# Fused block-causal attention and hash-routed experts on one core: V and rest casts moved to Pool, mask and rest-exponential work merged

## The chip, the cores and the metric

The kernel runs on one core of a Trainium2 chip (trn2). A core has a matmul engine (TensorE, PE in the profile, with its weight loads shown apart as PEld), a vector engine (VectorE, DVE), an activation engine (ScalarE, ACT), a programmable engine (GpSimd, POOL) and a queue engine for transfers (SyncE, SP). Each engine works through its own instructions strictly in program order, and engines wait for one another through semaphores. The metric is the device time of one execution in microseconds (us).

## The reference

Two stages follow each other. The first is block-causal attention over 8 batches of 8 heads, 576 positions and 64 dimensions per head; position blocks are 64 long, and a query sees its own block and all earlier ones. The second sends each of the 4608 resulting rows (512 wide, all heads of a position side by side) through one of 8 experts, chosen by a hash of its token id.

```
scores = scale * q @ k^T            # per batch and head, 576 x 576
scores = where(block_i >= block_j, scores, -1e9)
attn   = softmax(scores);  y = attn @ v
x      = y as [8*576 rows, 512]
e      = token_ids * 2654435761 % 8
out[row] = relu(x[row] @ w1[e]) @ w2[e]   # w1: 512 x 1024, w2: 1024 x 512
```

## The kernel before

**Attention.** Work goes in 32 pairs of heads, numbered g = 4*b + pr for batch b and pair pr. The 576 positions are 512 "main" positions, taken as four tiles of 128, and a "rest" of 64 (the last block). q, k and v come in as float32 by `load_qk` and `load_v` on SP's transfer queue (the first q and k partly on ACT's), into tiles `qf`, `kf`, `vf` with two buffers each. They are cast to bf16: q and k by `cast_qk` (L161) on DVE, two pairs at a time, and their rests of all heads at L174 in one cast; v by `cast_v` (L176) for one pair at a time. `cast_v` makes the four main tiles on DVE (L181, 128 partitions x 512 elements) and two "half block" tiles, which gather 64-row pieces on other partitions, on Pool (L182 and L183, 64 x 256 each). `cast_v4` (L185) puts the rest of V of the whole batch into `v4` on Pool (L189, twice 64 x 256). `vx` and `v4` have two buffers, chosen by the parity of the batch.

`T_pair` (L212) transposes q and k of one pair on PE and DVE copies the result (L231); `T_rest` (L195) does so for the rests of a whole batch. `S_chunk` (L270) makes one third of a pair's scores in PSUM and ACT takes their exponential (L286); there are two such PSUM buffers (`psS`). `mm_mask` (L257) adds a large negative number where a block may not be seen, by a rank-one matmul of `maskk` and `maskq`. For the key tile of half blocks (argument c true) it issues four matmuls of 64 x 64 tiles: two halves x of the output partitions times two heads m. `S_rest` (L288) makes the rest-by-rest scores of all heads of a batch: eight 64 x 64 matmuls, head m in PSUM bank m, and then two exponentials of 64 x 256 (L301), because the two heads lie in different banks. `PV` (L316) multiplies with V, 15 matmuls for each head of the pair; its PSUM tile has one buffer (`psO`). `norm` (L336) divides by the sums on DVE (L343, L346). `write_x` (L353) writes a finished batch to HBM in bf16 with five transfers that Pool issues (L356 four times, L358 once), since later rows are gathered by index.

**The order of the work** is written out by hand in the loop at L564 over g = 0 to 33. Iteration g has, in program order: the scores of pair g, interleaved with `PV` and `norm` of pair g-2; `T_pair(g + 2)`; `cast_v(g - 1)`, with `cast_v4` at the first pair of a batch (L588 to L592); one step of `steps`; a quarter of the casts of the next batch (L595 to L604), the q rest at pr 0, the k rest at pr 1 and `T_rest(b + 1)` at pr 2; at pr 1 `write_x(b - 1)`; then the loads: `load_qk(b + 2)`, and at pr 0 `load_v(b + 1)`. So V of pair g is cast in iteration g+1 and used by `PV` in iteration g+2.

**Routing** rides along in `steps`. Iterations 2 to 8 compute each token's slot, mainly on DVE. From iteration 10 each batch j has `place_a` at g = 10+2j (one-hot tiles `ohp` and `ohs` on DVE at L490 and L493, products `ohg` on Pool at L496 and L499) and `place_b` at g = 11+2j (five matmuls on PE at L509, which wait for `ohg`). Iterations 6 to 15 each clear one gather buffer on Pool (L612).

**Experts.** From L688 on, Pool gathers 128 rows at a time by index (L632), PE transposes them (L644) and does both matmuls (L656, L671), and Pool scatters the results (L678). A loop at L710 for rows over an expert's capacity comes last. Nothing in this part is edited.

Of the kernel before, what the change touches and what calls it, by code (L numbers as in the profile page):

```python
# [8 lines left out]
ACT = mybir.ActivationFunctionType  # L9
AX = mybir.AxisListType  # L10
F32 = mybir.dt.float32
BF16 = mybir.dt.bfloat16
# [8 lines left out]
B, H, S, D = 8, 8, 576, 64  # L21
# [3 lines left out]
NP = H // 2  # L25
# [4 lines left out]
NEG = -30000.0  # L30
SCALE = 1.0 / float(D) ** 0.5
# [3 lines left out]
def kernel(  # L35
# [10 lines left out]
    nc = tc.nc  # L46
    P = nc.NUM_PARTITIONS

    const = ctx.enter_context(tc.tile_pool(name="const", bufs=1))
# [9 lines left out]
    identbf = const.tile([P, P], BF16, name="identbf")  # L59
    lower = const.tile([P, P], BF16, name="lower")  # L60
    onesbf = const.tile([P, P], BF16, name="onesbf")
    maskk = const.tile([P, P], BF16, name="maskk")
    maskq = const.tile([P, P], BF16, name="maskq")
    perm3 = const.tile([P, NG], I32, name="perm3")
    xgs = [const.tile([P, DM], BF16, name=f"xg{z}") for z in range(2 * G)]
# [11 lines left out]
    nc.vector.memset(maskq[:], 0.0)  # L77
    for m in range(2):
        row = slice(64 * m, 64 * m + 1)
        nc.vector.memset(maskk[row, 96:128], NEG)  # L80
        nc.vector.memset(maskq[row, :], 1.0)

    att_ctx = ExitStack()
# [11 lines left out]
    def load_qk(b, h0=0, h1=H, rest=True, main=True, engs=None):  # L95
        if b not in loaded:
            loaded[b] = [ld.tile([P, 36, D], F32, name="qf", tag="qf"),
                         ld.tile([P, 36, D], F32, name="kf", tag="kf"), None]
        for w, src in ((0, q), (1, k)):
            t = loaded[b][w]  # L100
            eng = engs[w] if engs else nc.sync
            if main and w == 0:
                eng.dma_start(
                    t[:, 4 * h0 : 4 * h1, :].rearrange("p (h c) d -> p h (c d)", c=4),
                    src[b, h0:h1, 0:512, :].rearrange("h (p c) d -> p h (c d)", c=4),
                )
            elif main:
                for r in range(2):
                    eng.dma_start(
                        t[:, 4 * h0 : 4 * h1, :].rearrange(  # L110
                            "p (h r c) d -> p h r (c d)", r=2, c=2)[:, :, r],
                        src[b, h0:h1, 256 * r : 256 * r + 256, :].rearrange("h (p c) d -> p h (c d)", c=2),
                    )
            if rest:
                for g in range(2):
                    eng.dma_start(
                        t[64 * g : 64 * g + 64, 32:36, :],
                        src[b, 4 * g : 4 * g + 4, 512:576, :].rearrange("h r d -> r h d"),
                    )
# [18 lines left out]
    for z in range(2):  # L138
        vx = fix.tile([P, H, 6, D + 1], BF16, name=f"vx{z}")
# [21 lines left out]
    def cast_qk(b, which, r0=0, r1=NP, rest=True):  # L161
        src = loaded[b][which]
        cb = casted.setdefault(b, {})
        if which not in cb:
            cb[which] = att.tile([P, 36, D], BF16, name="qb" if which == 0 else "kb",
                                 tag="qb" if which == 0 else "kb")
        dst = cb[which]
        if r1 > r0:
            nc.vector.tensor_copy(  # L169
                dst[:, 8 * r0 : 8 * r1, :].rearrange("p (r c m) d -> p r m c d", c=4, m=2),  # L170
                src[:, 8 * r0 : 8 * r1, :].rearrange("p (r m c) d -> p r m c d", c=4, m=2),
            )
        if rest:
            nc.vector.tensor_copy(dst[:, 32:36, :], src[:, 32:36, :])  # L174

    def cast_v(b, pr):  # L176
        vf = loaded[b][2]
        vx, v4 = vexts[b % 2]
        hs = slice(2 * pr, 2 * pr + 2)
        vm = vf[:, 0:32, :].rearrange("p (h s) d -> p h s d", h=H)  # L180
        nc.vector.tensor_copy(vx[:, hs, 0:4, 0:D], vm[:, hs])  # L181
        nc.gpsimd.tensor_copy(vx[0:64, hs, 4:6, 0:D], vm[0:64, hs, 0::2, :])  # L182
        nc.gpsimd.tensor_copy(vx[64:128, hs, 4:6, 0:D], vm[0:64, hs, 1::2, :])  # L183

    def cast_v4(b):  # L185
        vf = loaded[b][2]
        vx, v4 = vexts[b % 2]
        for m in range(2):
            nc.gpsimd.tensor_copy(  # L189
                v4[64 * m : 64 * m + 64, :, m, 0:D], vf[64 * m : 64 * m + 64, 32:36, :])  # L190
# [64 lines left out]
                )  # L255

    def mm_mask(ps, o0, c, n, last=False):  # L257
        for x in range(2 if c else 1):
            for m in range(2):
                rows = slice(64 * m, 64 * m + 64)  # L260
                prt = slice(64 * x, 64 * x + 64) if c else slice(0, P)
                nc.tensor.matmul(  # L262
                    ps[prt, m, o0 : o0 + 128 * n].rearrange("p (t h j) -> p t h j", h=2, j=16)[:, :, 0, :],
                    lhsT=maskk[rows, 64:128] if c else maskk[rows, :],
                    rhs=maskq[rows, 0 : 64 * n].rearrange("p (t j) -> p t j", j=16),
                    start=False, stop=last,
                )


    def S_chunk(g, ch):  # L270
        b, pr = divmod(g, NP)
        ps = psS.tile([P, 2, 512], F32, name="ps", tag="ps")
        if ch < 2:
            mm_pair(b, pr, ps, 0, ch, 128, 448, first=True)
            mm_pair(b, pr, ps, 448, 3 - ch, 512, 64)
            mm_mask(ps, 0, False, 1, last=True)
        else:
            mm_pair(b, pr, ps, 256, 2, 384, 128, first=True)
            mm_pair(b, pr, ps, 384, 3, 384, 128)
            mm_mask(ps, 256, False, 2)  # L280
            mm_c(b, pr, ps, 0, 0)
            mm_c(b, pr, ps, 128, 1)
            mm_mask(ps, 0, True, 2, last=True)
        pt = pts[g % 3]
        ptv = pt[:, 0 : 2 * PTW].rearrange("p (m n) -> p m n", m=2)
        nc.scalar.activation(ptv[:, :, 512 * ch : 512 * ch + 512], ps[:], ACT.Exp, scale=SCALE)  # L286

    def S_rest(b):  # L288
        qk = qkTs[b]
        ps = psS.tile([P, 2, 512], F32, name="ps", tag="ps")  # L290
        for pr in range(NP):
            for m in range(2):
                rows = slice(64 * m, 64 * m + 64)
                nc.tensor.matmul(
                    ps[rows, m, 64 * pr : 64 * pr + 64],
                    lhsT=qk[rows, pr, 1, 512:576], rhs=qk[rows, pr, 0, 512:576],
                    start=True, stop=True,
                )
        for m in range(2):
            rows = slice(64 * m, 64 * m + 64)  # L300
            nc.scalar.activation(pt4s[b % 2][rows, 0 : NP * 64], ps[rows, m, 0 : NP * 64],  # L301
                                 ACT.Exp, scale=SCALE)


    PVS = [
# [239 lines left out]
    load_v(0)  # L545
    nc.sync.dma_start(tid[:], moe_token_ids.rearrange("(b s) -> b s", b=B))
    load_qk(1)
    rgen = route()
    for w in range(2):
        cast_qk(0, w, 0, 1, rest=False)  # L550
# [7 lines left out]
    steps = {g: (lambda: next(rgen, None)) for g in range(2, 9)}  # L558
    steps[7] = rows
    for j in range(B):  # L560
        steps[10 + 2 * j] = lambda j=j: place_a(j)
        steps[11 + 2 * j] = lambda j=j: place_b(j)
    steps[26] = placed
    for g in range(NPAIRS + 2):  # L564
        b, pr = divmod(g, NP)
        live = g < NPAIRS
        nxt = live and b + 1 < B
        if live:
            S_chunk(g, 0)
        if g >= 2:  # L570
            PV(g - 2, 0)
        if live:
            S_chunk(g, 1)
        if g >= 2:
            PV(g - 2, 1)
            norm(g - 2)
        if live:
            S_chunk(g, 2)
            if pr == 0:
                S_rest(b)  # L580
        if g == 0:
            T_pair(1)
        if g < 2:
            for w in range(2):
                cast_qk(0, w, g + 2, g + 3, rest=False)
        if g + 2 < NPAIRS:
            T_pair(g + 2)
        if g >= 1 and g - 1 < NPAIRS:  # L588
            bv, pv = divmod(g - 1, NP)
            cast_v(bv, pv)  # L590
            if pv == 0:
                cast_v4(bv)  # L592
        if g in steps:
            steps[g]()
        if nxt:  # L595
            if pr == 0:
                cast_qk(b + 1, 0, 0, 2)
            elif pr == 1:
                cast_qk(b + 1, 1, 0, 2)
            elif pr == 2:  # L600
                T_rest(b + 1)
                cast_qk(b + 1, 0, 2, 4, rest=False)
            else:
                cast_qk(b + 1, 1, 2, 4, rest=False)  # L604
        if pr == 1 and b >= 1:
            write_x(b - 1)
        if pr == (1 if b == 0 else 0) and b + 2 < B:
            load_qk(b + 2)
        if pr == 0 and b + 1 < B:
            load_v(b + 1)  # L610
        if 6 <= g < 6 + 2 * G:
            nc.gpsimd.memset(xgs[g - 6][:], 0.0)  # L612
        if pr == 0 and b == 6:
            load_w1(0)
        if pr == 0 and b == 7:
            load_w2(0)
# [161 lines left out]
```

The softmax here doesn't subtract the row's maximum and nothing guards it: scores larger than these inputs give would overflow.

## Time and profile before

Three runs took 359.70, 360.88 and 363.28 us; the median is 360.88 us. The profiled execution took 360.49 us, with a span of 358.9 us in the trace.

| engine | busy us | share of the span | instructions |
|---|---|---|---|
| PE | 281.0 | 78% | 3311 |
| PEld | 205.7 | 57% | 3311 |
| DVE | 169.5 | 47% | 390 |
| ACT | 148.9 | 41% | 177 |
| POOL | 178.8 | 50% | 265 |

The shares mix two stages with different limits. The exponentials of the attention stage start at 9.71 us and the last one ends at about 173 us; the first transposes of the experts' stage follow at 195 us, and from there PE is busy nearly without a break. What the change touches lies in the first 173 us, so the views used below are cut to stretches of that stage: a row of such a view gives, for one stretch, each engine's busy time in us with the number of instructions in brackets, the mean TensorE clock that was granted (1.00 is full), the share of the DMA engines' time and the rate in GB/s. In a timeline row the columns are start, duration, engine, line, operation, the tiles written and read, and how often; the bracket at the end says how long the engine had been idle before it and who released it.

### The profile page before, as it was taken

Reading aid. Unit: us, or ns where it says so; the run is one execution under the profiler, and the core shown is the slowest. Engines: PE = TensorE matmul, PEld = TensorE weight load, DVE = VectorE, ACT = ScalarE, POOL = GpSimd, SP = SyncE. Lnnn points to the kernel's source line nnn. Section 1 sums busy time; section 2 is a strip of 40 time slices with the busy share of each in tenths; the row PEclk is TensorE's granted clock in tenths of the full one; section 3 lists DMA queues with packets and bytes.
Section 4 is the critical chain, followed back from the end, with each engine's and each line's share of the span. In section 5 each row is a group of like instructions: output and inputs, shape, how many; then the busy total and the mean of one; then the engine's idle time right before and its main releaser. Section 6 shows DMA issues by size and latency. Waiting matters only on the chain. (4 is left out here: it accounts for less than half of the span.)

```text
span 358.9 us, 8081 instructions
## 1 busy us (share of the span) xinstructions
PE 281.0 (78%) x3311; PEld 205.7 (57%) x3311; DVE 169.5 (47%) x390; ACT 148.9 (41%) x177; POOL 178.8 (50%) x265
## 2 busy tenths in 40 slices
PE   2566768878686968697405998999999999999992
PEld 1344545656465746465303985776859494958640
DVE  5346779788588797854402013223231304141231
ACT  1453654767485768658200641231406050413200
POOL 2132075284929294945147356637373737523252
PEclk9997886989899899969855999999999999999997
DMA  6999981989787990982023799687988879644631
GB/s 197 295 269 270 277 212 45 288 218 265 180 221 187 250 202 22 243 186 50 22 66 94 152 215 201 216 151 234 175 228 178 209 197 213 190 104 119 147 138 71
DMA packets 67046, 64.59 MB, mean 180 GB/s; under 512 B 19378, under 2 KB 60340, under 8 KB 64960
## 3 DMA queue, kind: packets, MB, share of 16 engines
q0 software_dynamic: 12288, 35.71, 41.2%
q1 hardware_dynamic: 52064, 27.17, 30.0%
q10 hardware_dynamic: 2656, 1.18, 1.2%
q8 instruction: 26, 0.43, 0.5%
q14 instruction: 12, 0.10, 0.1%
HBM read 67.15 MB, written 15.20 MB: 229 GB/s over the span
## 5 line engine op out<-in xcount | busy, mean ns | idle before, releaser
L286 ACT ACTIVATE pt<-ps 128x1024 bf16<-128x1024 f32 x96 | 97.5, 1023 | 63.6 <-PE ps L262 60.2
L661 ACT ACTIVATE hT<-hp 128x640 bf16<-128x640 f32 x64 | 45.0, 703 | 117.2 <-PE hp L656 117.2
L656 PE MATMUL hp<-xT,w1b 128*128 128x320 bf16 x512 | 72.3, 302 | 0.7 <-DMA w1b<-in_moe_w_dram 0.5
L656 PEld LDWEIGHTS <-w1b 128*128 128x128 bf16 x512 | 69.8, 145 | 3.1 <-DMA w1b<-in_moe_w_dram 0.6
L671 PE MATMUL yp<-w2b,hT 128*128 128x512 bf16 x320 | 70.2, 379 | 0.0
L326 PE MATMUL O<-vx,pt 128*128 128x65 bf16 x896 | 47.2, 205 | 23.9 <-POOL vx L183 13.7
L678 POOL DMA_INDIRECT out_dram<-ysb,perm x40 | 39.7, 992 | 35.7 <-DVE ysb L676 26.9
L326 PEld LDWEIGHTS <-pt 128*128 128x128 bf16 x896 | 37.7, 104 | 29.8 <-issue 24.2
L645 DVE COPY xT<-tpx 128x512 bf16<-128x512 bf16 x40 | 15.7, 421 | 79.7 <-PE tpx L644 77.7
L676 DVE COPY ysb<-yp 128x512 f32<-128x512 f32 x40 | 27.7, 692 | 51.7 <-PE yp L671 51.7
L671 PEld LDWEIGHTS <-hT 128*128 128x128 bf16 x320 | 31.0, 98 | 36.2
L632 POOL DMA_INDIRECT xg<-x_dram,perm x40 | 40.6, 1016 | 16.6 <-issue 11.9
L356 POOL DMA_DIRECT2D x_dram<-xs x32 | 23.3, 733 | 40.5 <-DVE xs L346 40.0
L238 PE MATMUL ps<-qkT 64*128 64x64 bf16 (+2 forms) x384 | 39.5, 289 | 3.5 <-ACT pt L286 3.1
L644 PE MATMUL tpx<-identbf,xg 128*128 128x128 bf16 x160 | 15.1, 229 | 20.2 <-DMA xg<-x_dram,perm 16.9
L262 PE MATMUL ps<-maskq,maskk 64*128 64x64 bf16 (+2 forms) x320 | 30.1, 230 | 0.0
L346 DVE TENSOR_TENSOR xs<-O,rs 128x320 bf16<-128x320 f32 x64 | 28.4, 486 | 1.6 <-DVE rs L343 0.4
L182 POOL CAST vx<-vf 64x256 bf16<-64x256 f32 x32 | 15.1, 473 | 23.3 <-DMA vf<-in_v_dram 22.4
L231 DVE COPY qkT<-tp 128x1024 bf16<-128x1024 bf16 x32 | 22.1, 689 | 9.1 <-PE tp L226 9.1
L644 PEld LDWEIGHTS <-xg 128*128 128x128 bf16 x160 | 10.9, 101 | 24.1 <-DMA xg<-x_dram,perm 18.4
L226 PE MATMUL tp<-identbf,qb 128*128 128x128 bf16 x128 | 14.6, 246 | 8.0 <-DVE qb L169 8.0
L496 POOL TENSOR_TENSOR ohg<-ohs,vhi 128x360 bf16<-128x360 bf16 x8 | 8.5, 1060 | 23.9 <-DVE ohs L493 23.7
(110 smaller groups left out, 271.3 us busy)
## 6 DMA issues: line engine op xcount, KB each, us to landing
vf<-in_v_dram SPq DMA_DIRECT2D x16, 512.0 KB, 6.9
w1b<-in_moe_w_dram POOLq DMA_DIRECT2D x8, 1024.0 KB, 8.8
w2b<-in_moe_w_dram POOLq DMA_DIRECT2D x8, 1024.0 KB, 8.1
qf<-in_q_dram SPq DMA_DIRECT2D x7, 1024.0 KB, 6.4
kf<-in_k_dram SPq DMA_DIRECT2D x14, 512.0 KB, 6.5
x_dram<-xs POOLq DMA_DIRECT2D x32, 128.0 KB, 5.1
qf<-in_q_dram SPq DMA_DIRECT2D x16, 64.0 KB, 5.6
vf<-in_v_dram SPq DMA_DIRECT2D x16, 64.0 KB, 5.5
```

The source lines that it names most:

```text
L238: nc.tensor.matmul(ps[:, m, o0 : o0 + n], lhsT=qk[rows, pr, 1, 128 * kt : 128 * kt + 128], rhs=qk[rows, pr, 0, q0 : q0 + n], start=first, ...
L262: nc.tensor.matmul(ps[prt, m, o0 : o0 + 128 * n].rearrange("p (t h j) -> p t h j", h=2, j=16)[:, :, 0, :], lhsT=maskk[rows, 64:128] if c e ...
L286: nc.scalar.activation(ptv[:, :, 512 * ch : 512 * ch + 512], ps[:], ACT.Exp, scale=SCALE)
L326: nc.tensor.matmul(O[:, t, :], lhsT=pt[:, m * PTW + o0 : m * PTW + o0 + 128], rhs=vx[:, h, i, :], start=(n == 0), stop=(n == t),)
L346: nc.vector.tensor_tensor(out=xs[:, :, 0:DM].rearrange("p t (d h k) -> p h t d k", d=4, h=H)[:, h], in0=O[:, m, :, 0:D].rearrange("p t (k ...
L632: nc.gpsimd.indirect_dma_start(out=xgs[g % (2 * G)][:], out_offset=None, in_=x_dram[:, :], in_offset=bass.IndirectOffsetOnAxis(ap=perm3[:, ...
L644: nc.tensor.transpose(out=tp[:, db, :], in_=xg[:, db * P : (db + 1) * P], identity=identbf[:])
L656: nc.tensor.matmul(hp[:, t, 0:HC], lhsT=w1b[:, db, ft::NFT], rhs=xT[:, db, t * HC : (t + 1) * HC], start=(db == 0), stop=(db == NKT - 1),)
L661: nc.scalar.activation(hT[:, ft, :].rearrange("p (t n) -> p t n", t=2), hp[:, :, 0:HC], ACT.Relu)
L671: nc.tensor.matmul(yp[:], lhsT=hT[:, ft, tt * P : (tt + 1) * P], rhs=w2b[:, ft, :], start=(ft == 0), stop=(ft == NFT - 1),)
L676: nc.vector.tensor_copy(ysb[:], yp[:])
L678: ins = nc.gpsimd.indirect_dma_start(out=out[:, :], out_offset=bass.IndirectOffsetOnAxis(ap=perm3[:, gg : gg + 1], axis=0), in_=ysb[:], in ...
```

## The change

It has five parts.

1. The main V cast and both rest casts (q and k) go from DVE to Pool.
2. `cast_v` runs five pairs ahead of its `PV` rather than one: iteration g casts pair g+3, iteration 0 casts pairs 0 to 3. The half-block casts are done for two pairs at a time, at even pairs (64 x 512 elements instead of twice 64 x 256). `load_v` follows: V of batch 1 is loaded with the first loads, and V of batch b+2 right behind q and k of batch b+2.
3. The mask of the half-block key tile takes two matmuls of 64 x 128 tiles instead of four of 64 x 64: `maskk` gets a second plane that has the negative number in columns 32 to 64 and 96 to 128.
4. The rest scores of both heads go into one PSUM bank on different partitions, so that one exponential of 128 x 256 replaces two of 64 x 256.
5. `place_a` and `place_b` move one iteration later (`place_a` at g = 11+2j, `place_b` at 12+2j, `placed` at 27).

It is meant to take work off DVE, to take V's casts out of the way of `PV`, and to shorten the small work on PE and ACT.

```diff
-    maskk = const.tile([P, P], BF16, name="maskk")
+    maskk = const.tile([P, 2, P], BF16, name="maskk")
...
-        nc.vector.memset(maskk[row, 96:128], NEG)
+        nc.vector.memset(maskk[row, 0, 96:128], NEG)
+        nc.vector.memset(maskk[row, 1, 32:64], NEG)
+        nc.vector.memset(maskk[row, 1, 96:128], NEG)
...
         if rest:
-            nc.vector.tensor_copy(dst[:, 32:36, :], src[:, 32:36, :])
+            nc.gpsimd.tensor_copy(dst[:, 32:36, :], src[:, 32:36, :])
...
-        nc.vector.tensor_copy(vx[:, hs, 0:4, 0:D], vm[:, hs])
+        nc.gpsimd.tensor_copy(vx[:, hs, 0:4, 0:D], vm[:, hs])
+        if pr % 2:
+            return
+        hs = slice(2 * pr, 2 * pr + 4)
         nc.gpsimd.tensor_copy(vx[0:64, hs, 4:6, 0:D], vm[0:64, hs, 0::2, :])
         nc.gpsimd.tensor_copy(vx[64:128, hs, 4:6, 0:D], vm[0:64, hs, 1::2, :])
...
-        for x in range(2 if c else 1):
-            for m in range(2):
-                rows = slice(64 * m, 64 * m + 64)
-                prt = slice(64 * x, 64 * x + 64) if c else slice(0, P)
-                nc.tensor.matmul(
-                    ps[prt, m, o0 : o0 + 128 * n].rearrange("p (t h j) -> p t h j", h=2, j=16)[:, :, 0, :],
-                    lhsT=maskk[rows, 64:128] if c else maskk[rows, :],
-                    rhs=maskq[rows, 0 : 64 * n].rearrange("p (t j) -> p t j", j=16),
-                    start=False, stop=last,
-                )
+        for m in range(2):
+            rows = slice(64 * m, 64 * m + 64)
+            nc.tensor.matmul(
+                ps[:, m, o0 : o0 + 128 * n].rearrange("p (t h j) -> p t h j", h=2, j=16)[:, :, 0, :],
+                lhsT=maskk[rows, c, :],
+                rhs=maskq[rows, 0 : 64 * n].rearrange("p (t j) -> p t j", j=16),
+                start=False, stop=last,
+            )
...
-                    ps[rows, m, 64 * pr : 64 * pr + 64],
+                    ps[rows, 0, 64 * pr : 64 * pr + 64],
                     lhsT=qk[rows, pr, 1, 512:576], rhs=qk[rows, pr, 0, 512:576],
-                    start=True, stop=True,
+                    start=(pr == 0), stop=(pr == NP - 1),
                 )
-        for m in range(2):
-            rows = slice(64 * m, 64 * m + 64)
-            nc.scalar.activation(pt4s[b % 2][rows, 0 : NP * 64], ps[rows, m, 0 : NP * 64],
-                                 ACT.Exp, scale=SCALE)
+        nc.scalar.activation(pt4s[b % 2][:, 0 : NP * 64], ps[:, 0, 0 : NP * 64], ACT.Exp, scale=SCALE)
...
     load_qk(1)
+    load_v(1)
...
-        steps[10 + 2 * j] = lambda j=j: place_a(j)
-        steps[11 + 2 * j] = lambda j=j: place_b(j)
-    steps[26] = placed
+        steps[11 + 2 * j] = lambda j=j: place_a(j)
+        steps[12 + 2 * j] = lambda j=j: place_b(j)
+    steps[27] = placed
...
-        if g >= 1 and g - 1 < NPAIRS:
-            bv, pv = divmod(g - 1, NP)
-            cast_v(bv, pv)
-            if pv == 0:
-                cast_v4(bv)
+        for gv in range(NP) if g == 0 else (g + 3,):
+            bv, pv = divmod(gv, NP)
+            if bv < B:
+                cast_v(bv, pv)
+                if pv == 0:
+                    cast_v4(bv)
...
         if pr == (1 if b == 0 else 0) and b + 2 < B:
             load_qk(b + 2)
-        if pr == 0 and b + 1 < B:
-            load_v(b + 1)
+            load_v(b + 2)
```

More of the change, by code (lines that the diff above doesn't have):

```diff
@@ L275, in S_chunk @@
             mm_pair(b, pr, ps, 448, 3 - ch, 512, 64)
-            mm_mask(ps, 0, False, 1, last=True)
+            mm_mask(ps, 0, 0, 1, last=True)
         else:
@@ L279, in S_chunk @@
             mm_pair(b, pr, ps, 384, 3, 384, 128)
-            mm_mask(ps, 256, False, 2)
+            mm_mask(ps, 256, 0, 2)
             mm_c(b, pr, ps, 0, 0)
             mm_c(b, pr, ps, 128, 1)
-            mm_mask(ps, 0, True, 2, last=True)
+            mm_mask(ps, 0, 1, 2, last=True)
         pt = pts[g % 3]
```

## The prediction

> **What bounds the kernel now.** First the page's slices, to see which stage the change touches.
>
> ```profile
> PE   2566768878686968697405998999999999999992
> POOL 2132075284929294945147356637373737523252
> PEclk9997886989899899969855999999999999999997
> ```
>
> One slice is 9 us. From the 23rd digit on PE is full; that is the experts' stage, which is not edited. The first 19 are attention: PE is mostly at six to nine tenths, and the granted clock falls to 6 and 8 now and then. The times of L286 on ACT, three per pair, date the iterations, and I cut the span there: iterations 0 to 9, 10 to 26 (those with routing's placement), 27 to 31, and the remainder.
>
> ```profile
> 9.71:69.41 59.70, 41.92 (x668) 29.58 (x665) 40.44 (x107) 32.18 (x37) 17.68 (x42) 0.86 0.95 235
> 69.41:150.59 81.18, 62.83 (x1248) 48.48 (x1249) 65.64 (x145) 54.73 (x61) 55.26 (x88) 0.94 0.81 200
> 150.59:173.07 22.48, 17.07 (x332) 12.82 (x332) 12.35 (x32) 15.71 (x17) 12.11 (x24) 0.85 0.55 120
> 173.07:358.87 185.80, 156.51 (x1051) 113.33 (x1049) 45.90 (x87) 44.99 (x64) 91.95 (x99) 0.93 0.65 159
> ```
>
> Only the first three rows, 163.4 us, can move; the last, 185.8 us, shifts as a block. In the long middle row no engine is full (DVE 65.6 of 81.2), so the waits of PE from 70 to 157 us come next.
>
> ```profile
> PE O L326 <- POOL vx L183: 12.4, 7, 3.3
> PE O L326 <- DVE vx L181: 4.2, 11, 0.7
> PE pq L509 <- POOL ohg L499: 2.3, 4, 0.6
> ```
>
> `PV` waits 16.6 us for V casts. The longest wait is in Pool's timeline:
>
> ```profile
> 88.87 1.30 POOL L189 CAST v<-vf 64x256 bf16<-64x256 f32 x2
> 90.12 2.79 POOL L356 DMA_DIRECT2D x_dram<-xs  x4
> 92.90 0.56 POOL L358 DMA_DIRECT2D x_dram<-xs  x1
> ...
> 94.67 0.95 POOL L183 CAST vx<-vf 64x256 bf16<-64x256 f32 x1
> 95.71 0.78 POOL L496 TENSOR_TENSOR ohg<-ohs,vhi 128x360 bf16<-128x360 bf16 x1
> ```
>
> Once per batch `write_x` holds Pool for 3.4 us, the next cast stands behind it, and PE stands 3.3 us with a half-clock spell after it. So each batch has three iterations of about 4.2 us and one of 5.5 to 7.9 us, 19.1 us in all (81.18 / 17 x 4).
>
> **What the Trainium skill says.** (1) "SBUF — State Buffer", Who interferes with whom: DVE casts between SBUF tiles (two-port mode) and GpSimd work exclude each other, and the loser blocks for the whole instruction. The trace agrees largely: in the row at 88.87 above two casts take 1.30 us beside DVE casts, against 0.86 alone. Over all rows Pool's and DVE's SBUF work overlaps by 21.9 us, and there Pool's rows are 9.9 us and DVE's 6.7 us above their shortest: 76% of a full exclusion. (2) "GPSIMD Engine Reference", Elementwise — side-by-side cycle accounting: about 1.8 cycles per element, 768 ns for 512 elements. The trace agrees for 256 elements:
>
> ```profile
> L182 POOL CAST vx<-vf x32: 388/400/1005, 16.5 to 170.7; 64x256 bf16<-64x256 f32 x32
> L181 DVE CAST vx<-vf x32: 419/421/622, 23.7 to 175.1; 128x512 bf16<-128x512 f32 x32
> ```
>
> (3) "TensorE: Matmul & The Clock Gate", What's actually happening: an idle window of some 3.4 us halves the clock. The clock of 0.86 and 0.85 above fits.
>
> **The change part by part.** *V casts off `PV`'s path.* Five pairs ahead, about 20 us, covers a 3.4 us hold of Pool: the 16.6 us of waits go. That is what PE gains if nothing else takes their place.
>
> *DVE.* It loses 4 x 0.42 us (L181) and two rests (0.88 + 0.43 us in the batch from 112.96 to 132.05) per batch, 3.0 us; its 15.4 to 15.8 us of busy time per batch become 12.5. DVE is then no bound.
>
> *Pool per batch.* Main casts of 128 x 512: from the page's 0.77 us to twice L182, 0.80 us; I take 0.80, four are 3.2 us (0.77 leads to 0.1 less). Half-block casts: four of 64 x 512, also 0.80, 3.2 us (as before: eight of 0.40). `cast_v4` 0.9. Two rests of 256 elements at 0.40, 0.8. `ohg` four times 0.78, 3.1. `write_x` 3.4. Some 18 starts, each 0.05 later than the end before (0.39 to 0.40 us casts start every 0.45), 0.9. Sum 15.5 us. The port comes on top. Below: nothing. Above: all 5.6 us of DVE's remaining SBUF work per batch (four L169 at 0.69, two L490 at 0.82, two L493 at 0.6) block Pool, 21.1 us. In the batch from 112.96 us Pool's 7.6 us of casts and products were stretched by some 1.5 us, 20%, beside 8.7 us of such DVE work; 5.6 / 8.7 of that on 11.2 us is 1.4. I take **16.9 us per batch**.
>
> *Who waits for Pool.* Not `PV` any more, but two others. `ohg` feeds `place_b` one iteration later, twice a batch. The k rest, behind V's casts, `cast_v4` (which waits for `PV` of the same iteration) and `ohg`, feeds `T_rest` one iteration later; PE's next scores are queued behind both. So Pool has no slack beyond an iteration, and the middle stretch goes at Pool's pace, not at PE's own. PE's own is 3.04 us (iteration 29, no long wait) to 3.4 us (iteration 9), or with `place_b` and `T_rest` some 14 us per batch. With clearing of six buffers (0.57 us each, 3.4 us, half of it taken as hidden in Pool's waits for `ohs`): 17/4 x 16.9 + 1.7 = 73.5 us against 81.2, **7.7 us gained**.
>
> *Iterations 27 to 31.* No placement is left and Pool has little to do. 22.5 us, with two iterations at half clock, become 5 x 3.4 = 17.0: **5.5 us gained**.
>
> *Iterations 0 to 9.* One new wait: Pool's k rest of batch 1 now stands behind the casts of V of batch 1, whose data end a wait at 30.04 us. Then 0.8 + 1.6 + 0.9 + 0.4 us and gaps: 33.9 us, while `T_rest(1)` now starts at 31.29: 2.6 us lost. Against that DVE, which paces several of these iterations with routing, is freed of L181 (waits of PE for it before 70 us: 2.7 us) and of a rest ahead of a needed cast: some 0.4 us in iteration 1. Sum **+0.5 us**, bounded by -2.6 and +3.1.
>
> *Mask and rests.* Two mask matmuls of 64 x 128 (L262, ahead of L250) start 0.15 us before the next work, four of 64 x 64 the same: nothing gained, at most 0.1 us per pair. One exponential instead of two saves ACT 0.37 us per batch; ACT is busy 12.9 of 19 us, so it is hidden. The loads move in order only: 3.5 MB per batch in 16.9 us are 209 GB/s, and the early slices show 270 to 295.
>
> Sum: 7.7 + 5.5 + 0.5 = 13.7 us, 360.9 - 13.7 = **347.2 us**.
>
> **The rivals.** *Pool is cheaper than that (0.20).* If the port costs nothing, 15.5 us per batch and buffers cleared in idle time: 66 us, gain 15.3; with the 5.5 and 0.5, **339.6 us**. For it: the records of port stretches are a minority of rows. Against: 11 us of Pool's port work per batch beside 5.6 on DVE leave little room. If Pool also ran so far ahead that PE set the pace, 60 us would do, 333 us in all; nothing in the rows has Pool that fast.
>
> *Port blocking eats the gain (0.12).* Half of DVE's work blocks Pool: 18.3 us per batch, 79.5 us, gain 1.7; the tail gains 3.5 and the start loses 2.6: **358.3 us**, no change. For it: L183 at 0.95 and L496 up to 1.2 us on average in one batch.
>
> *Pool becomes a worse bound than the waits were (0.08).* All of it blocks: 21.1 us per batch, 91.4 us, 10.2 lost; start 2.6 lost, tail 3 gained: **370.7 us**. For it: the same exclusion, with every cast now on one side. Against: 76% at most was seen, shared between both engines.
>
> **How the numbers follow.** My forecast has 0.60. The range leaves out the two cases on the slow side (0.20) and takes in the cheap Pool and some of what lies beyond: 337 to 356 us. Faster by over 1% (below 357.3): 0.60 + 0.20 and a quarter of the third case, 0.83; within 1%: 0.09; slower: 0.08.
>
> **What would show it.** Right: no waits of `PV` for `vx`; Pool busy 16 to 17 us in each batch of the middle stretch with hardly an idle row; PE waiting for L499 and for the k rest instead; casts of 128 x 512 at 0.80 us; the first `T_rest(1)` near 34 us; iterations 27 to 31 at 3.4 us. Wrong: casts far from 0.80 us, a middle stretch at PE's 14 us per batch, or a load of V that now comes late because its buffer is freed by Pool.

## The result, and the profile after

The changed kernel took 345.63 us (median of 4 runs, 344.91 to 346.88) against 360.38 us for the kernel before on the same chip. The ratio is 0.958, 95% interval 0.952 to 0.964. The forecast was 347.2 us, faster. Ratios, here and below, leave out slow executions, those over 1.5% above the fastest of the same kernel (among them two of six in experiment 10 and two of four in experiment 12).

The span fell from 358.9 to 343.6 us. First the slices of the page after:

```profile
PE   1574784998878888895039989999999999999991
POOL 3065378388988789960374647274664737232352
PEclk9997886999989899997558999999999999999998
```

One slice is now 8.6 us. PE is full from the 22nd digit on, at 180 us, where it was the 23rd, at 197 us; the first transposes of the experts' stage start at 174.2 us, and before at 189.7 us (not 195). Pool's row through attention is mostly eights and nines where it was uneven. The span is cut by the same exponentials (L289 now) into iterations 0 to 9, 10 to 26, 27 to 31 and the remainder. The columns are length, busy time of PE, PEld, DVE, ACT and Pool with instruction counts, mean granted clock, DMA share and GB/s.

```profile
9.96:69.13 59.17, 40.26 (x653) 28.33 (x650) 39.45 (x94) 30.59 (x34) 31.11 (x59) 0.86 1.04 249
69.13:141.48 72.35, 62.73 (x1219) 46.45 (x1216) 58.47 (x121) 51.05 (x56) 62.66 (x94) 0.95 0.92 218
141.48:157.51 16.03, 14.79 (x332) 11.24 (x330) 10.29 (x24) 14.86 (x16) 9.72 (x15) 1.00 0.65 135
157.51:343.60 186.09, 156.78 (x1042) 113.60 (x1038) 45.60 (x86) 44.99 (x64) 91.93 (x99) 0.93 0.65 160
```

| stretch | before | forecast | after | change |
|---|---|---|---|---|
| iterations 0 to 9 | 59.7 | 59.2 | 59.2 | -0.5 |
| iterations 10 to 26 | 81.2 | 73.5 | 72.4 | -8.8 |
| iterations 27 to 31 | 22.5 | 17.0 | 16.0 | -6.5 |
| remainder | 185.8 | 185.8 | 186.1 | +0.3 |

With 0.25 us more before the first exponential, that is the whole 15.3 us of span. The waits of PE in the middle stretch (69 to 141 us), all that are listed:

```profile
PE pq L509 <- POOL ohg L499: 8.0, 8, 1.7
PE tp L231 <- DVE kb L171: 1.0, 3, 0.3
PE O L326 <- DVE qkT L212: 0.4, 1, 0.4
```

The 16.6 us for `vx` are gone; `ohg` has grown from 2.3 to 8.0 us and is met at all eight `place_b`. Pool's own waits in the same stretch, and its timeline around one of them with the `write_x` after it:

```profile
POOL ohg L496 <- DVE ohs L493: 8.2, 5, 2.8
```

```profile
121.82 1.10 POOL L496 TENSOR_TENSOR ohg<-ohs,vhi 128x360 bf16<-128x360 bf16 x1 [2.81 <-DVE ohs L493]
122.88 0.78 POOL L499 TENSOR_TENSOR ohg<-ohs,vlo 128x360 bf16<-128x360 bf16 x1
123.61 0.39 POOL L176 CAST kb<-kf 128x256 bf16<-128x256 f32 x1
123.95 2.87 POOL L356 DMA_DIRECT2D x_dram<-xs  x4
126.81 0.56 POOL L358 DMA_DIRECT2D x_dram<-xs  x1
127.37 1.18 POOL L183 CAST vx<-vf 128x512 bf16<-128x512 f32 x2
```

The 3.4 us hold by `write_x` is still there. Before the product at 121.82 us Pool stood idle for 2.81 us, with `place_b` of the coming iteration waiting for the result. At five of the eight places it is so: Pool is free and `ohs` comes last. At the other three (95.66, 112.94 and 130.65 us) Pool comes last, busy without a wait since `write_x`. The longest of PE's waits, 1.7 us, is at the first of these. DVE's `ohs` there, then Pool's rows:

```profile
93.14 0.94 DVE L493 TENSOR_TENSOR ohs<-iota_p,shi 128x360 bf16<-128x360 bf16 x1
```

```profile
94.61 0.96 POOL L188 CAST vx<-vf 64x512 bf16<-64x512 f32 x1
95.66 0.78 POOL L496 TENSOR_TENSOR ohg<-ohs,vhi 128x360 bf16<-128x360 bf16 x1
```

The product starts 1.58 us after the end of `ohs` here and 0.57 and 0.56 us at the other two, where it is 0.15 us when Pool is free. The costs of Pool's casts, all forms that the change made:

```profile
L183 POOL CAST vx<-vf x32: 602/623/1092, 16.5 to 146.3; 128x512 bf16<-128x512 f32 x32
L187 POOL CAST vx<-vf x16: 611/751/1222, 17.1 to 144.9; 64x512 bf16<-64x512 f32 x16
```

(The three numbers are the shortest, the median and the longest, in ns.)

### The profile page after: what moved, and what is told of

It is laid out like the page before. It is cut to its first block, busy times and chain, and to the rows that moved or that the text cites. A ratio compares the mean times of both kernels' runs of the same rounds, so it can differ in the third digit from the quotient of the medians.

```text
span 343.6 us, 7894 instructions
## 1 busy us (share of the span) xinstructions
PE 277.1 (81%) x3247; PEld 201.2 (59%) x3247; DVE 158.8 (46%) x346; ACT 142.8 (42%) x169; POOL 198.1 (58%) x281
## 5 line engine op out<-in xcount | busy, mean ns | idle before, releaser
L289 ACT ACTIVATE pt<-ps 128x1024 bf16<-128x1024 f32 x96 | 94.3, 1022 | 54.3 <-PE ps L265 54.0
L633 POOL DMA_INDIRECT xg<-x_dram,perm x40 | 40.6, 1015 | 16.5 <-issue 11.9
L326 PE MATMUL O<-vx,pt 128*128 128x65 bf16 x896 | 43.7, 206 | 2.6 <-DVE xs L346 2.2
L243 PE MATMUL ps<-qkT 64*128 64x64 bf16 (+2 forms) x384 | 37.9, 280 | 2.6 <-ACT pt L289 2.2
L326 PEld LDWEIGHTS <-pt 128*128 128x128 bf16 x896 | 35.8, 105 | 6.4 <-issue 1.8
L183 POOL CAST vx<-vf 128x512 bf16<-128x512 f32 x32 | 21.1, 669 | 20.9 <-DMA vf<-in_v_dram 19.9
L265 PE MATMUL ps<-maskq,maskk 64*128 64x64 bf16 (+1 forms) x256 | 28.3, 214 | 0.0
L531 POOL DMA_DIRECT2D w1b<-in_moe_w_dram x8 | 4.9, 614 | 30.8 <-PE tpx L645 26.7
L231 PE MATMUL tp<-identbf,qb 128*128 128x128 bf16 x128 | 13.7, 233 | 8.2 <-DVE qb L171 8.0
```

Source lines behind the costliest of these rows:

```text
L243: nc.tensor.matmul(ps[:, m, o0 : o0 + n], lhsT=qk[rows, pr, 1, 128 * kt : 128 * kt + 128], rhs=qk[rows, pr, 0, q0 : q0 + n], start=first, ...
L265: nc.tensor.matmul(ps[:, m, o0 : o0 + 128 * n].rearrange("p (t h j) -> p t h j", h=2, j=16)[:, :, 0, :], lhsT=maskk[rows, c, :], rhs=maskq ...
L326: nc.tensor.matmul(O[:, t, :], lhsT=pt[:, m * PTW + o0 : m * PTW + o0 + 128], rhs=vx[:, h, i, :], start=(n == 0), stop=(n == t),)
L633: nc.gpsimd.indirect_dma_start(out=xgs[g % (2 * G)][:], out_offset=None, in_=x_dram[:, :], in_offset=bass.IndirectOffsetOnAxis(ap=perm3[:, ...
```

## The experiments

Twelve runs in three groups, each group on one chip beside its own runs of the kernel before, which took 372.3 us (the first four below), 361.0 us (the next four) and 379.2 us (the last four). On the first and third chip the remainder, nearly all of it the experts' stage, which no edit touches, takes 199 to 207 us where it takes 186 or 187 on the others; so across groups the ratio and the lengths of the three attention stretches are compared, not the total. For the changed kernel itself three profiles give 59.2, 61.4 and 60.5 us for iterations 0 to 9, 72.4, 71.8 and 72.1 us for 10 to 26, and 16.02 us each time for 27 to 31: that is the scatter to hold each stretch against. Each experiment has one profile.

One thing helps to read the middle stretch. Its even iterations, with `place_b` in all but the first, take 44.8 to 45.2 us together in the three profiles, the odd ones 26.9 to 27.5. Each of the three profiles has one or two odd iterations at a granted clock of 0.50 to 0.73, which take 4.03 to 5.04 us instead of 3.10, some 2 us in all.

**1. `place_b` one iteration later (what is the pace of the middle stretch?).**

```diff
-    for j in range(B):
-        steps[11 + 2 * j] = lambda j=j: place_a(j)
-        steps[12 + 2 * j] = lambda j=j: place_b(j)
-    steps[27] = placed
+    def place(j):
+        if j > 0:
+            place_b(j - 1)
+        if j < B:
+            place_a(j)
+
+    for j in range(B + 1):
+        steps[11 + 2 * j] = lambda j=j: place(j)
+    steps[28] = placed
```

`place_b(j)` now comes two iterations after `place_a(j)`, and `placed` moves by one; everything else, Pool's work too, is the same.

> place_b of batch j runs two iterations after its place_a, in the same step ahead of place_a of batch j+1. Theory A (the middle stretch is paced by the chain transposes - DVE copy and one-hot tiles - Pool products - place_b, which has one iteration to fit in): the 8.0 us of PE waiting for ohg go, the middle stretch falls from 72.4 to 62-65 us, in all 336 to 339 us. Theory B (the prediction: Pool's own sum of work, 15.5 to 16.9 us per batch, is the pace): Pool has no time to win, the waits move to the k rest and the total stays at 343 us or above.

Measured: ratio 0.957 (0.950 to 0.964); iterations 10 to 26 in 68.4 us, 3.7 below the mean of the three profiles above. Waits of PE there, the two longest, and Pool's wait for `ohs`:

```profile
PE tp L206 <- POOL kb L176: 2.9, 4, 1.2
PE tp L231 <- issue: 1.4, 2, 1.0
```

```profile
POOL ohg L496 <- DVE ohs L493: 2.3, 3, 1.3
```

The waits for `ohg` are gone and Pool waits 2.3 us where it waited 8.2. Pool does the same work in 3.7 us less, so its sum was not what paced the stretch: the chain from `T_pair`'s copy over `ohp` and `ohs` on DVE and `ohg` on Pool to `place_b` on PE, which had to fit into one iteration, was. The 62 to 65 us of that theory did not come, though: the gain is half of the least it promised, and PE now waits for the k rest, as the other theory had it. Pool is busy for 64.6 of these 68.4 us, so its work is not far behind as a limit. The total doesn't show the gain: the ratio is that of the changed kernel, within the intervals. Iterations 0 to 9 took 61.7 us in this profile, 1.3 more than the mean of the three, which is a part of the reason; the rest is open, as the changed kernel was not run on this chip.

**2. The main V cast back on DVE, still five pairs ahead (is the engine or the lead what matters?).**

```diff
-        nc.gpsimd.tensor_copy(vx[:, hs, 0:4, 0:D], vm[:, hs])
+        nc.vector.tensor_copy(vx[:, hs, 0:4, 0:D], vm[:, hs])
```

> The 128 x 512 cast of V goes back to DVE, still five pairs early. Theory A: PE waits for ohs, which stands on DVE; 0.42 us more per iteration on DVE lengthens the chain by at most 0.4 us per two iterations, and Pool's port work falls; 343 to 349 us. Theory B (Pool's sum is the pace): 2.4 us less on Pool per batch, so about 2 us less per batch over four batches, 336 to 340 us. A rival, that the gain came from taking work off DVE: it is lost, 355 us or more.

Measured: ratio 0.969 (0.962 to 0.976). The middle stretch took 69.5 us, the start 64.4 us. The row of the middle stretch, then PE's and Pool's longest waits in it:

```profile
74.37:143.84 69.47, 60.60 (x1219) 44.84 (x1220) 63.62 (x139) 51.08 (x56) 51.89 (x78) 1.00 0.92 225
```

```profile
PE pq L509 <- POOL ohg L499: 7.1, 8, 1.0
```

```profile
POOL ohg L496 <- DVE ohs L493: 16.4, 8, 3.0
```

Taking 10.8 us off Pool shortens the middle by 2.6 us, and `ohg` is still waited for at all eight places, now always with `ohs` last. The even iterations take 44.7 us together, as in the changed kernel; the 2.6 us lie in the odd ones, all at full clock here. Again Pool's sum is not the limit, and nor is the engine of the main cast what mattered in the middle: with it on DVE and the lead kept, the stretch is no longer than with it on Pool. What the move to Pool does bring is the start: with the cast on DVE, iteration 2 takes 14.3 us instead of 10.3, since DVE, with the transposes' copies queued on it, stands at a cast of V whose data have not come. DVE's longest wait before 75 us:

```profile
DVE vx L183 <- DMA vf<-in_v_dram: 6.4, 1, 6.4
```

**3. The Pool casts without the lead.** One pair at a time (the half-block casts too, 64 x 256 again), one pair ahead of `PV`, V loaded where the kernel before loads it; the rest of the change stays.

```diff
-        if pr % 2:
-            return
-        hs = slice(2 * pr, 2 * pr + 4)
...
-    load_v(1)
...
-        for gv in range(NP) if g == 0 else (g + 3,):
-            bv, pv = divmod(gv, NP)
-            if bv < B:
-                cast_v(bv, pv)
-                if pv == 0:
-                    cast_v4(bv)
+        if g >= 1 and g - 1 < NPAIRS:
+            bv, pv = divmod(g - 1, NP)
+            cast_v(bv, pv)
+            if pv == 0:
+                cast_v4(bv)
...
-            load_v(b + 2)
+        if pr == 0 and b + 1 < B:
+            load_v(b + 1)
```

> All casts stay on Pool, but V is cast one pair ahead of its use again, per pair, and loaded as in the kernel before. If the five pairs of lead are what removed the waits: PV waits for vx on Pool again, 12 us or more in the middle stretch, and the total is 358 to 370 us. If the relief of DVE was what counted: 348 us or less.

Measured: ratio 1.036 (1.029 to 1.042), slower than the kernel before. Row of the middle stretch, PE's longest wait in it, Pool's longest:

```profile
66.10:161.31 95.21, 70.27 (x1214) 51.95 (x1211) 54.69 (x121) 52.20 (x56) 63.12 (x110) 0.80 0.70 174
```

```profile
PE O L323 <- POOL vx L185: 19.7, 8, 4.3
```

```profile
POOL ohg L493 <- DVE ohs L490: 30.1, 8, 5.2
```

Without the lead, the middle takes 95.2 us, 14 more than before: now all of V stands behind `write_x` and `ohg`. The move to Pool alone loses; the lead, with the loads and the larger casts that come with it, is worth 23 us on top of it. Part of this is time at a lower clock: iterations 11, 15, 19 and 23 take 7.8 to 8.8 us at a mean clock of 0.60 or 0.61.

**4. Mask and merged exponential undone together.** Both functions as before the change; casts, lead and placement stay.

```diff
-        nc.scalar.activation(pt4s[b % 2][:, 0 : NP * 64], ps[:, 0, 0 : NP * 64], ACT.Exp, scale=SCALE)
+        for m in range(2):
+            rows = slice(64 * m, 64 * m + 64)
+            nc.scalar.activation(pt4s[b % 2][rows, 0 : NP * 64], ps[rows, m, 0 : NP * 64],
+                                 ACT.Exp, scale=SCALE)
```

(and the rest scores of head m in bank m and the four mask matmuls, as in the diff's removed lines).

> The mask of the half-block tile back to four 64 x 64 matmuls and the rest exponentials back to two of 64 x 256. The prediction has both at nothing: within 0.3% of the changed kernel, 344.5 to 346.5 us. A rival, that they matter where ACT is the pace (iterations 27 to 31 and the odd ones at 3.1 us): up to 0.37 us per batch and 0.1 us per pair, 348 to 350 us.

Measured: ratio 0.962 (0.956 to 0.968), not told apart from the changed kernel by its time. But iterations 27 to 31 took 15.63 us instead of 16.02, and the undisturbed odd iterations 3.00 or 3.01 us instead of 3.10. Undoing the edit seemed to help there; experiment 10 takes the mask alone.

**5. The changed kernel once more**, as the yardstick of the second group.

> The changed kernel itself, beside the others on one chip. Its ratio to the kernel before should be 0.958 or, on a chip whose experts' stage is slower, a little nearer to 1 (15 us of 372 us is 0.960).

Measured: 346.6 us, ratio 0.960 (0.952 to 0.968).

**6. Rests ahead of V's casts on Pool.** The q rest at pr 0 and the k rest at pr 1 are issued first in Pool's part of the iteration instead of last.

```diff
+        if nxt and pr < 2:
+            cast_qk(b + 1, pr, 0, 0)
         for gv in range(NP) if g == 0 else (g + 3,):
...
-                cast_qk(b + 1, 1, 0, 2)
+                cast_qk(b + 1, 1, 0, 2, rest=False)
```

> The changed kernel with the q and k rest casts ahead of V's casts on Pool. If T_rest(1) waits only because the k rest of batch 1 stands behind the casts of V of batch 1, that wait (2.0 us in the changed kernel's trace, 2.6 us in the prediction) goes and iterations 0 to 9 take 2 us less; the middle stretch stays within 1 us. Rival: the wait is for the data of k itself or DVE's routing fills the gap, then less than 0.7 us is gained.

Measured: 341.6 us, ratio 0.947 (0.940 to 0.955). The k rest of batch 1, in Pool's timeline of the changed kernel (its first profile) and then of this one:

```profile
29.58 0.97 POOL L183 CAST vx<-vf 128x512 bf16<-128x512 f32 x1 [6.10 <-DMA vf<-in_v_dram]
...
32.77 0.40 POOL L176 CAST kb<-kf 128x256 bf16<-128x256 f32 x1
```

```profile
28.37 0.39 POOL L176 CAST kb<-kf 128x256 bf16<-128x256 f32 x1
30.52 0.62 POOL L183 CAST vx<-vf 128x512 bf16<-128x512 f32 x1 [1.76 <-DMA vf<-in_v_dram]
```

The rest no longer stands behind the wait for V's data, and the wait of PE for it (2.0 us at L206) is gone: iteration 2 fell from 10.4 to 8.5 us. The start as a whole fell to 56.1 us, 5.3 below the run beside it and 3.1 below the lowest of the three profiles. Iterations 4, 6 and 8, where routing runs on DVE, shortened too, by 0.8, 1.5 and 1.2 us; no wait in the trace names why, so this part of the gain stays unexplained. The middle stretch fell by 2.0 us: iteration 17, which in the run beside it ran at a clock of 0.50 and took 5.04 us, takes 3.10 us at full clock. Why the clock did not fall here is not shown.

**7. Both: `place_b` later and rests first** (the edits of 1 and 6).

> Both edits, place_b two iterations after place_a and the rests first. In the run with place_b later PE still waited 2.9 us for k rests in the middle stretch and 2 to 3 us at the start; without these 4 to 7 us less than the changed kernel if the waits are real, 4 us or less if Pool and DVE are full anyway and the waits only move.

Measured: 337.4 us (335.7 to 338.3), ratio 0.933 (0.926 to 0.941): 9.2 us faster than the changed kernel on the same chip. Start 55.4, middle 69.0, tail 16.5 us.

**8. Most of Pool's main V casts left out** (edit of 1; the casts of batches 2 to 7 are not made, so attention there uses the V of batches 0 and 1 for the main tiles).

```diff
-        nc.gpsimd.tensor_copy(vx[:, hs, 0:4, 0:D], vm[:, hs])
+        if b < 2:
+            nc.gpsimd.tensor_copy(vx[:, hs, 0:4, 0:D], vm[:, hs])
```

> place_b later, and the 128 x 512 casts of V left out from batch 2 on (the attention of these batches uses the V of batches 0 and 1). Theory: with the waits for ohg gone, Pool's and DVE's work on their shared port sets the pace (Pool 64.6 and DVE 60.3 of 68.4 us busy). Then taking 10.7 us of casts from Pool lets the middle stretch fall to 60-63 us, and DVE's q and k casts to 0.70-0.75 us each from 0.85-1.01. Rival: PE's own work is the pace, then the stretch stays at 66 us or more.

Measured (two runs): 342.0 us, ratio 0.948, middle stretch 68.8 us. The 60 to 63 us that I expected did not come, nor the shorter casts of q and k on DVE (0.86 and 0.80 us); the stretch is as long as in experiment 1, which has all the casts. Iterations 10 to 21 are quicker (44.4 against 47.8 us), and then two iterations of 6.8 and 5.9 us take it back. Pool's longest wait, and PE's behind it:

```profile
POOL vx L188 <- DMA vf<-in_v_dram: 7.3, 2, 4.8
```

```profile
PE tp L207 <- POOL kb L176: 5.5, 3, 2.8
```

A faster Pool runs into the loads: V's data come too late, and the k rest queued behind that cast holds the transposes. This is not yet a limit on what the loads can do: experiments 11 and 12 get the same loads through in stretches of 65.0 and 63.6 us.

**9. The changed kernel a third time**, yardstick of the third group.

> The changed kernel once more, as the yardstick for the three beside it. Expected: 0.958 of the kernel before; iterations 27 to 31 at 16.0 us and iterations without placement at 3.10 us each.

Measured: ratio 0.965 (0.961 to 0.969); tail 16.02 us, its undisturbed iterations 3.10 to 3.11 us each, as expected.

**10. The mask alone undone**: the four matmuls of 64x64 tiles again, merged exponential kept.

> The changed kernel with only the mask's edit undone: four matmuls of 64x64 tiles again for the half-block key tile; the merged exponential of the rests stays. Theory of the prediction: the mask's form is worth nothing, so the time and iterations 27 to 31 (16.0 us) stay within 0.1 us. Rival, from the run with mask and exponential undone together, where iterations 27 to 31 took 15.6 us and the shortest odd iteration 3.01 us instead of 3.10: two matmuls of 64x128 tiles cost PE about 0.1 us per pair more than four of 64x64, so the odd iterations 27 and 29 take 3.0 us, iterations 27 to 31 some 15.6 us, and the whole 0.4 to 2 us less than the changed kernel.

Measured: ratio 0.947 (0.943 to 0.950), against 0.965 (0.961 to 0.969) for the run beside it: this kernel is the faster. The spans of the two profiles are 7.1 us apart. Of these, 0.4 us lie in iterations 27 to 31 (15.64 against 16.02 us), where no clock drop disturbs either profile. Another 2.1 lie in the middle. The undisturbed odd iterations take 3.00 or 3.01 us instead of 3.10 there, but the even ones take that back; what is left is iterations 17 and 25, which ran at a lower clock in the run beside it. Their rows there, then here:

```profile
99.16:103.22 4.06, 4.06 (x72) 3.06 (x71) 2.06 (x5) 2.96 (x3) 2.97 (x5) 0.72 0.88 201
133.10:137.21 4.11, 4.11 (x72) 3.11 (x71) 2.35 (x5) 2.97 (x4) 3.23 (x6) 0.70 0.83 130
```

```profile
97.46:100.46 3.00, 3.00 (x74) 2.31 (x72) 2.12 (x5) 2.87 (x3) 2.88 (x6) 1.00 1.17 262
130.61:133.61 3.00, 3.00 (x74) 2.31 (x71) 2.11 (x5) 2.87 (x3) 2.88 (x5) 1.00 0.58 66
```

Another 1.9 us lie in the start and 3.3 in the experts' stage. That the mask's edit causes any of this beyond the 0.4 us is not shown, and experiment 4, which undoes it too, had no better total than the changed kernel. Where the two forms differ can be read in PE's timeline. The changed kernel, then this one, from the mask of 128 columns to the transposes of the next pair (L265 and L267 are the mask, L255 the scores of the half-block tile):

```profile
149.82 0.22 PE L265 MATMUL ps<-maskq,maskk 64*128 64x128 bf16 x2
149.97 0.30 PE L255 MATMUL ps<-qkT 64*64 64x128 bf16 x8
150.21 0.23 PE L265 MATMUL ps<-maskq,maskk 64*128 64x128 bf16 x2
150.37 0.40 PE L231 MATMUL tp<-identbf,qb 128*128 128x128 bf16 x4
```

```profile
146.79 0.22 PE L267 MATMUL ps<-maskq,maskk 64*128 64x128 bf16 x2
146.94 0.31 PE L255 MATMUL ps<-qkT 64*64 64x128 bf16 x8
147.08 0.23 PE L267 MATMUL ps<-maskq,maskk 64*64 64x128 bf16 x4
147.24 0.40 PE L231 MATMUL tp<-identbf,qb 128*128 128x128 bf16 x4
```

From the start of L255's group to that of L231's it is 0.40 us with two mask matmuls and 0.30 us with four. The four have the tile form of the scores before them, 64x64, and start 0.14 us after these began; the two have another, 64x128, and start 0.24 us after. What follows them starts 0.16 us later in both. So the two have one change of form more, and it comes with 0.10 us. The Trainium skill has a reason, "TensorEngine Tiling (Array Packing)", Tiling Modes: a change of the tiling mode, not of the tile, drains the engine. The page has no figure for it. The trace agrees with its 0.10 us, but no run here tells a drain from another cost of the change.

**11. Experiment 7 with the four mask matmuls.**

> The version with place_b moved behind the next iteration's start and the rests ahead of V's casts on Pool, and the mask as four matmuls again. If the mask's two matmuls cost 0.1 us per pair and PE is now what paces the middle stretch, this is 1 to 3 us faster than that version with two matmuls (ratio 0.933 before): about 0.927. If the form of the mask is worth nothing, 0.933 again.

Measured: ratio 0.932 (0.927 to 0.937) against 0.933 in experiment 7, on another chip: not told apart by ratio. The middle stretch is 65.0 us instead of 69.0, but one profile of each can't separate the mask from experiment 7's one idle window of 2.5 us, which has no named cause. It beats both kernels of its group: 26 us faster than the one before and 13 faster than the changed one.

**12. As 11, with Pool's main V casts of odd pairs of batches 2 to 7 on DVE.**

```diff
-        nc.gpsimd.tensor_copy(vx[:, hs, 0:4, 0:D], vm[:, hs])
+        eng = nc.vector if b >= 2 and pr % 2 else nc.gpsimd
+        eng.tensor_copy(vx[:, hs, 0:4, 0:D], vm[:, hs])
```

> As the run with the four mask matmuls beside it, with the main V cast of the odd pairs of batches 2 to 7 on DVE, so that Pool and DVE share the work. If Pool still sets the pace (1.3 us of casts less per batch), the middle stretch falls by 2 to 5 us. If PE and the transfers set it, nothing changes (within 1 us), or DVE's copies for PE come later and it is 1 to 3 us slower.

Measured: 354.4 us (350.9 to 359.4) against 353.0 us (351.4 to 355.5) for 11: no difference to be told. Pool's busy time in the middle fell from 62.8 to 57.6 us and the stretch from 65.0 to 63.6 us, less than the 2 to 5 us of a Pool that sets the pace.

## Why the prediction was right, and where its working was not

The forecast of 347.2 us was 1.6 us high. The stretches are each within 1.2 us of the forecast. But two steps inside the longest one failed, Pool's work 2 us per batch too dear and a wait of 2 us per batch left out. That they are of one size is luck.

**V off `PV`'s path: right.** No wait for `vx` is left. Experiment 3 shows that this is the lead's doing: with the casts on Pool but late, the stretch is 95.2 us; and experiment 2 has the lead with the main cast on DVE, and 69.5 us.

**"The middle stretch goes at Pool's pace": the length right, the reason wrong.** It took 17.0 us per batch (72.35 / 17 x 4), forecast 16.9 and a little for clearing. But Pool was busy only 14.7, 15.5, 14.4 and 14.8 us in the four batches from 72.43 us on:

```profile
72.43:89.12 16.69, 14.45 (x291) 10.69 (x291) 14.37 (x32) 12.04 (x13) 14.66 (x23) 1.00 1.11 274
89.12:107.37 18.25, 15.41 (x291) 11.33 (x289) 13.67 (x30) 12.04 (x13) 15.54 (x25) 0.91 0.99 246
107.37:125.08 17.71, 15.52 (x292) 11.45 (x289) 13.94 (x30) 12.04 (x14) 14.42 (x22) 0.90 0.97 235
125.08:141.48 16.40, 14.14 (x291) 10.51 (x289) 13.77 (x30) 11.96 (x13) 14.81 (x23) 1.00 0.53 105
```

The "hardly an idle row" did not hold: Pool idled 8.2 us for `ohs`, some 2 us per batch, and its mean of 14.9 with these 2 makes 16.9 of the 17.3 us that these four batches take on average. The working had named the wait of `place_b` for `ohg` but put its length down to Pool's queue. Experiments 1, 2, 8 and 12 speak against the queue as the pace: the same Pool work goes into 68.4 us once `place_b` has two iterations, and taking casts from Pool gains 2.6 us (in the odd iterations, which ran at full clock), nothing and 1.4 us. The queue has a part all the same: at three of eight products Pool came 0.4 to 1.4 us later than a free Pool would have.

**Casts at 0.80 us: too dear.** They take 0.61 us when nothing disturbs them, and so do the 64x512 casts; a 256-element cast takes 0.39. So the cost is about 0.17 us and 0.86 ns per element, not proportional, and doubling L182's 0.40 doubled the fixed part with it. The 768 ns of the Trainium skill ("GPSIMD Engine Reference", Elementwise) seemed to confirm it, but they belong to its 1.8 cycles per element. The same section gives 1.03 cycles for the simplest loop bodies, by estimate 0.86 ns at the page's 1.2 GHz, and that is the slope measured here. With port stretches eight casts came to 5.8 us per batch (four L183 at 656 ns, two L187 at 861, two L188 at 704 in the middle stretch); without, they would be 4.9, where the sum had 6.4. A second mis-sized term is the 0.9 us for starts: the small gaps between Pool's rows, those under 0.12 us, come to 0.3 us per batch.

**The port: right in size.** By the mean against the shortest row in the middle stretch, Pool's casts and products are stretched by about 1.7 us per batch (0.2 on L183, 0.7 on L187 and L188, 0.2 on the q rest, 0.6 on L496), forecast 1.4. The 76% of a full exclusion was misread: the 9.9 and 6.7 us count all rows of the casts and products, and the rows that do overlap are 8.7 and 5.7 us above their shortest, 66% of the 21.9 us. The half that was left out is DVE's: its casts at L171 took 0.83 us instead of 0.69, L490 0.91 instead of 0.82, L493 0.70 instead of 0.6, and its busy time per batch is 13.9 us, not 12.5. DVE is no bound by its sum, as said, but it is in the chain that `ohg` waits for.

**Iterations 27 to 31: right,** 16.0 against 17.0: the pace is 3.10 us, nearer the 3.04 us than the 3.4 that I took. Here too it is the lead: without it, in experiment 3, they take 24.0 us.

**The start: right in size, in part by luck.** `T_rest(1)`'s transposes started at 33.2 us (forecast 33.9), and PE waits 2.0 us for that k rest (forecast 2.6). Not foreseen: iteration 6 grew from 7.3 to 9.5 us, with routing's operations on DVE stretched beside Pool (L432 took 1.08 us against 0.40, L433 1.33 against 0.61). Iterations 3 and 7 gave most of it back (0.9 and 1.8 us shorter). The three profiles range from 59.2 to 61.4 us, so a hit to within 0.1 us means little. In the middle stretch the k rest, said to be the second wait, is not among PE's waits at all; it appears once `ohg` is out of the way (experiment 1).

**"Nothing gained" by the mask: wrong in sign.** It costs 0.1 us per pair where PE paces, the outer edge of the bound given. The step that failed is the comparison "four of 64 x 64 the same": it priced the mask by its distance to the next work and left out the distance to the work before.

**One exponential instead of two: hidden, as said.** Experiment 4 has two again and experiment 10 one, and iterations 27 to 31 took 15.63 and 15.64 us. **Loads: right** for this change; experiment 8 shows that a faster Pool can run into a late one.

The rivals: the cheap Pool was half right, in the casts and not in the stretch, because Pool's sum did not set the time. A port that eats the gain or makes Pool worse than the waits is excluded by the 72.4 us.

## What to carry to other kernels

Work moved to an idle engine pays only with its lead: in the middle stretch the casts on Pool cost 14 us when issued just in time and saved 9 when issued five pairs early, past the engine's longest hold. The lead was worth as much there with the main cast left on DVE. After that, look for the chain that has only one iteration to cross three engines, and give it a second one before taking work off any of them; and put a small cast that others wait for ahead of one that may stand at a load. On PE, look at the tile form of the neighbours before merging small matmuls: here two in a different form took 0.10 us longer than four in the same.

## What the runs showed that was not expected

- Two 64x128 mask matmuls after eight 64x64 scores take 0.10 us longer than four 64x64 ones, until the next work starts; the 0.10 us stand before the first of them, where the tile form changes.
- Pool's f32-to-bf16 casts follow 0.17 us and 0.86 ns per element of a partition (0.39 us for 256, 0.61 for 512, the two sizes seen), the same on 64 and 128 partitions.
- The order of two short casts on Pool was worth 5.1 us of 346.6, more than the cast itself takes in all eight batches (8 x 0.39 us for the k rest), in part by one wait for a load and by a clock drop that did not happen. Which idle window lets the clock fall stays open: iteration 16 took 5.97 us in the changed kernel, where iteration 17 then ran at 0.64, and 5.94 us in experiment 6, where it ran at 1.00; PE's longest wait in it was 1.7 us in both.
